# RWKV attention and SoLU feed-forward on one core: w_out's column mean taken by fp32 products of TensorE, more transposes given to DMA, and a new order of work

## The chip, the core and the metric

The kernel runs on one core of a Trainium2 chip. The core has five engines with queues of their own: PE (TensorE, matrix products; its weight loads are shown as PEld), DVE (VectorE), ACT (ScalarE), POOL (GpSimd) and SP (SyncE, which here only issues transfers). Each works through its instructions in order and waits on semaphores for the others. Products go to PSUM, which has eight banks of 512 fp32 columns by 128 partitions; everything else lies in SBUF. Transfers (DMA) are issued from SP, ACT or POOL and run on 16 DMA engines. The metric is the device time in microseconds (us) of one execution; smaller is better.

## The reference

Per batch b (4) and head h (8), over 768 steps with head size 48, a decaying state is read and updated; its output, as 3072 rows of 384, goes through a hidden layer of 1024 with a softmax-weighted activation, a layer norm with gain g, and an output product:

```python
for t in range(S):
    cur = np.einsum('bhd,bhe->bhde', u[None] * kt, vt)
    y[:, :, t] = np.einsum('bhd,bhde->bhe', rt, state + cur)
    state = wt[:, :, :, None] * state + np.einsum('bhd,bhe->bhde', kt, vt)
...
h = x @ w_in
e = np.exp(h - h_max)
sm = e / (np.sum(e, axis=-1, keepdims=True) + 1e-09)
solu = h * sm
ln = (solu - mu) / np.sqrt(var + 1e-06) * g_ln
return (ln @ w_out).astype(np.float32)
```

## The kernel before

The 768 steps are cut into 6 chunks of 128, so there are 24 units (chunk, batch), unit i being chunk i // 4 of batch i % 4. Each unit goes through the same stages, and one long string, ORDER (lines 21 to 65), says by hand-written or planned words in which order the instructions of all stages are recorded; each engine executes its own in that order. A word is a stage's letters, the unit and, after a point, an engine or a PSUM bank: `kr2.d` copies unit 2's transposed keys by DVE, `M3.0` takes unit 3's scores into bank 0. `InOrder` (line 70) keeps each engine to the order of the words, and also keeps the transfers issued from SP and ACT in one order; its line 86 records nearly all instructions, so nearly every row of the profile carries L86, and rows are told apart by what they write and read.

The stages of a unit, with the word and the line of the function:

- loads `LW`, `LK`, `LR`, `LV` (263 to 272) of w, k, r, v, 192 KB each, without a suffix from SP, with `.a` from ACT, with `.g` from POOL. Each input has a ring of seven tiles.
- `lw` (337), logarithm of w on ACT; `cum` (340), sums of it along time by two products on PE; `ex` (346), exponentials in PSUM on ACT; `kp` (350), k and r scaled by them on DVE.
- `krk`, `krr`, `kr` (388 to 394): the scaled k and r turned by eight transposes of PE and copied out of PSUM by ACT or DVE. For eleven units `kt` (398) turns them by one DMA from SP instead.
- `p`, `q`, `dg`, `dv` (354 to 375): the bonus term with u, on POOL with a sum on DVE. `vb` (367): v in bf16, on ACT or POOL.
- `M` (407), the scores, eight products; `m` (415), masked and copied out by DVE or ACT.
- `Y` (429), the output of the recurrence; with `i` the bonus is added by a product with the identity, with `n` by DVE in `y` (451), which copies it out (`.a` by ACT, `.d` by DVE). `S`, `et`, `st` (457 to 480): the state.
- `X`, `xT` (485 to 490): y turned by three transposes of PE and copied out by ACT or DVE; for seven units `xt` (401) turns it by one DMA from SP.
- `H` (497), the hidden layer, 24 products with w_in; `e` (515), exponential on ACT; `he` (527), product on DVE; `hq` (533), square on ACT; `Oa`, `Ob` (588, 592), products with w_out and the column sums for the norm; then `qm`, `lv`, `rs`, `o` and the store `out`. For four units the hidden layer is taken by rows and turned by `ht`.

Once, at the start, the weights are made ready. `LI` loads w_in in three parts, `wi` (303) casts each to bf16. `LO` loads w_out in two halves of four blocks. `gs`, `gc` (296, 300) turn and scale g. `gw` (307, `gain`) multiplies a block of w_out by g, eight times, all on ACT; `mn` (314) takes the mean over all rows of the result by eight bf16 products with a matrix of -1/1024; `ce` (322, `centre`) adds that to each block: on DVE from the fp32 block, g and the mean in PSUM in one operation, on POOL to the block already multiplied by g, from the mean that `mc` (319) has copied to SBUF. Six blocks are centred on DVE and two on POOL. Centred blocks are used first by `Oa0`. `hot` (329) issues products on zeros that keep PE active. `us` (289) spreads u over the partitions by the one fp32 product of 384 columns.

Of the kernel before, what the change touches and what calls it, by code (L numbers as in the profile page):

```python
# [8 lines left out]
F32 = mybir.dt.float32  # L9
BF16 = mybir.dt.bfloat16  # L10
# [8 lines left out]


ORDER = """
LU0 LR3.g LW3.a LW1.a LW2.g lw3 LR0.a cum3.0 LG0 ih0 ex3 LW0 gs0.7 LK3 LR2.g hot1.2 LV0.g ik0 LK0 lw1 lw0 LV3.g
gc0 cum0.4 LK2.a us0.6 p0 lw2 LW5.g ex0 kp3 LR1 kp0 cum1.0 cum2.2 krk3.7 krr3 uc0 ex2 q0 ex1 kp2 LK1 LR6.g kp1
krk0.6 LW4 krr0 krk2.5 krr2 kr0.a lw4 LR4.g vb0.a kr2.d vb3.a p1 M0.3 p3 LO0 LW6 dg0 M2.5 kr3.a LK4 m0.d lw5
hot10.1 LV1 LR5 LK6.a dv0 LK5.g m2.d LV2.a LO1 M3.0 S0.7 q3 gw2.a gw3.a hot1.4 LI1 q1 lw6 krk1.6 cum4.2 et0 LV4
m3.d p2 st0 cum6.0 dg3 gw0.a cum5.4 ex4 S3.7 gw1.a p4 kp4 q2 dv3 krr1 ex6 dg1 LV5.g krk4.3 krr4 ex5 vb1.a Y0.i2
kp6 kr4.d y0.a LI2 et3 X0.2 krk6.3 st3 p6 kr1.a vb2.a LW8 xT0.a kp5 krr6 LI0.a dg2 M1.0 krk5.7 krr5 kr6.a m1.d
S1.2 dv1 M4.4 dv2 Y3.i3 S2.6 gw4.a LK7 gw7.a et2 kr5.d LW7.g et1 m4.d hot1.7 y3.a q4 gw6.a Y1.i3 M6.0 gw5.a st2
Y2.i5 y1.a y2.a vb5.a mn0.4 X2.7 wi0.a vb4.a st1 m6.d wi1.p LR7.g M5.2 X1.0 S5.1 xT2.a S4.6 et5 p5 lw7 LR8.g dg4
ce4.d LK8 LV7 et4 ce2.d wi2.a xT1.d st5 LW10.a st4 X3.5 m5.d LR10.a cum7.0 mc0 ex7 xT3.a ce1.d H0.6 dv4 H1.2 kp7  # L30
LK9.g H3.0 e0 lw8 e1 ce0.d LK10.a he0 he1 lw10 H2.6 ce7.d hq0.a ce3.p krk7.5 ce5.p e3 LV9 e2 LK11 hq1.a ce6.d
Oa0.3 q6 he3 vb7.a krr7 Ob0 LW9.g LV6.g Y4.i4 q5 LV8.g LR9.a he2 dg5 LW11 cum10.1 cum8.6 y4.a Oa1.0 qm0 ex10 lv0
rs0 kr7.d ex8 kp10 LW13.g Ob1 krk10.4 o0.a hq3.a p8 kp8 p7 dv5 Y5.n5 qm1 LR11.g y5.d lv1 M7.2 X4.6 LW15.a m7.d
q7 krr10 LW17 dg7 kr10.d xT4.a q8 dg6 rs1 lw11 p10 Oa3.5 o1.a cum11.6 dg8 hq2.a H4.2 LW12 LR12.a ex11 lw9 kp11
out0 S7.0 et7 Ob3 dv7 Y7.n1 vb6.a out1 cum9.6 LR17 LK15.g Oa2.4 qm3 st7 vb8.p e4 Ob2 he4 lv3 dv6 LK14.g krk8.0
S6.2 X5.3 LK12.a LV10 krr8 LV12.g ex9 lw13 y7.d rs3 o3.a hq4.a kp9 lw12 qm2 Y6.i5 lv2 xT5.d X7.7 krk11.6 LV11
vb9.p out3 kr8.d krr11 LR13.g LW14.a cum12.0 et6 xT7.a y6.a rs2 LR14.g st6 M8.2 krk9.5 krr9 kr11.d ex12 m8.a
H5.6 o2.d out2 q10 M11.3 LK13 lw17 kp12 dv8 LR15 S8.0 kr9.d LV15.g M9.1 e5 m11.d Oa4.5 LW18 Ob4 m9.a sel8 he5
LV14 et8 X6.6 vb11.a M10.3 st8 xT6.d p9 lw14 cum14.1 LK17.g hq5.a ex14 qm4 lv4 m10.d cum13.6 ex13 hot2.0 q9 rs4
kp14 kp13 dg9 Y8.i0 o4.a LW21.g dg10 sel9 Oa5.4 cum17.1 S9.3 LR16 lw15 p11 ex17 S11.5 cum15.6 Ob5 kp17 y8.a p12  # L40
et9 qm5 ex15 lv5 kp15 st9 dv9 Y9.n0 q11 q12 y9.d et11 rs5 H6.1 X8.6 o5.a p13 vb12.a p14 st11 dg11 kt12 e6 out4
dv11 LK21.g H7.3 X9.5 xT8.a he6 e7 LR19.g hq6.a vb10.a H8.6 lw18 krk14.0 LV16 dg12 krr14 dv10 kt15 xT9.d out5
he7 M12.1 Oa6.5 LV13.g Y11.n4 m12.d kr14.a e8 Ob6 M15.0 y11.d qm6 LR18 hq7.a lv6 he8 rs6 m15.d H9.3 dv12 o6.a
# [3 lines left out]
lv8 vb13.p q13 e11 kp18 dv14 rs8 S15.2 o8.a S13.3 st12 e12 Oa9.0 dv15 he11 et15 lw21 LW20 Y15.n6 hq11.a et13
dg13 LV21 he12 Ob9 LV23.g LV19.g p18 st15 M13.4 LW23 y15.d qm9 dv13 kt16 cum21.1 hq12.a ex21 H10.6 lv9 p16 m13.d
st13 lw19 kp21 Y13.i4 Oa11.3 e10 rs9 o9.a out7 he10 q18 cum19.1 Ob11 dg18 qm11 lw20 Oa12.7 Ob12 ex19 LR22 q16
y13.a kp19 hq10.a M16.1 dg16 S14.5 lv11 Y14.n6 rs11 LV20.g X13.4 LV22.g out8 qm12 lv12 p17 m16.d xT13.d y14.d  # L50
o11.a lw22 S16.0 vb17.p et14 q17 dg17 rs12 st14 o12.a LR23 vb18.a cum20.1 p19 et16 ex20 ea10.p H13.3 q19 e13
# [49 lines left out]
def kernel(  # L101
# [16 lines left out]
    DM = H * D  # L118
    DF = moe_w_in.shape[1]
# [25 lines left out]
    def bank(shape, dtype, slot, name):  # L145
        size = 1
        for d in shape[1:]:
            size *= d
        first = int(slot) * 512
        if dtype == BF16:  # L150
            part = banks[:, first:first + size // 2].bitcast(BF16)
        else:
            part = banks[:, first:first + size]
        if len(shape) == 2:
            return part
        names = "abc"[:len(shape) - 1]
        return part.rearrange(f"p ({' '.join(names)}) -> p {' '.join(names)}", **dict(zip(names, shape[1:])))
# [467 lines left out]
    def store(i, x):  # L625
# [2 lines left out]

    stages = dict(
        ih=make_halves, ik=make_keep, LW=load_w, LK=load_k, LR=load_r, LV=load_v, LU=load_u, LG=load_g, LI=load_w_in, LO=load_w_out,  # L630
        us=spread_u, uc=copy_u, gs=turn_g, gc=copy_g, wi=cast_w_in, gw=gain, mn=column_mean, mc=copy_mean,
        ce=centre, hot=warm_up,
        lw=log_w, cum=cumulate, ex=decays, kp=scaled, p=bonus_rk, q=bonus_u, vb=v_cast, dg=bonus_sum, qh=bonus_half, dv=bonus_v,
        krk=transposed_k, krr=transposed_r, kr=transposed_copy, M=scores, m=scores_copy, sel=scores_mask,
# [41 lines left out]
```

## Time and profile before

| | |
|---|---|
| median of 3 runs | 144.75 us (144.69 to 145.68) |
| profiled execution | 145.05 us |
| its span, first to last instruction | 143.2 us |
| mean granted clock of TensorE | 0.995 |
| transfers turning k and r, y, hidden rows | 11, 7, 4 |
| HBM read, written | 22.03 MB, 4.72 MB |

The profile is of one execution. A group's row gives the instruction (what it writes <- what it reads), its count, the busy time and the mean ns of one, and then the idle time of its engine just before it and what ended that. A row in order of time gives start, length and the instruction. A waits row says which engine waited for whom. "The chain that ended last" follows the work back from the last instruction, at each step to what released it. Products on PE overlap: a row of 324 ns may start another every 160 ns, so the spacing of starts is the price of one and not its length. "Idle time" of an engine off the chain costs nothing by itself.

### The profile page before, as it was taken

What the parts mean: (1) busy time and instruction counts of PE and PEld (TensorE: products, weight loads), DVE (VectorE), ACT (ScalarE), POOL (GpSimd) and SP (SyncE); (2) the same over time, 40 slices, a digit from 0 to 9 for tenths busy, and PEclk for the clock granted to TensorE, in tenths of its full rate; (3) what the DMA queues carried; (4) which work ended last, traced back from release to release, by engine and by line L of the source; (5) the groups of instructions that cost most, each with busy time, mean ns of one, the idle gap of its engine ahead of it and who ended that gap; (6) DMA issues with size and microseconds to landing.
All of it is one profiled execution on the core that took longest, in us unless ns stands there. A gap on an engine that the chain in (4) does not pass through costs nothing.

```text
span 143.2 us, 4784 instructions
## 1 busy us (share of the span) xinstructions
PE 127.6 (89%) x1886; PEld 94.5 (66%) x1886; DVE 124.0 (87%) x206; ACT 122.2 (85%) x254; POOL 117.2 (82%) x150
## 2 busy tenths in 40 slices
PE   0597956988999999999999999996999999999980
PEld 0145445556967878678987797786778566687750
DVE  6048879979999999999999999999699999888480
ACT  3658799979999999999999989995787887887962
POOL 7999999999999999999999999999994753326000
PEclk9999999999999999999999999999999999999998
DMA  4999999999995999999998999996977863985325
GB/s 93 277 297 347 313 287 381 384 267 240 287 299 118 250 273 314 255 263 163 211 268 215 271 201 252 195 256 99 169 165 80 223 128 79 142 213 180 115 80 197
DMA packets 86488, 31.67 MB, mean 221 GB/s; under 512 B 80153, under 2 KB 84258, under 8 KB 86466
## 3 DMA queue, kind: packets, MB, share of 16 engines
q1 hardware_dynamic: 69330, 20.62, 66.6%
q0 software_dynamic: 2432, 7.47, 16.4%
q10 hardware_dynamic: 14704, 3.28, 10.5%
q8 instruction: 14, 0.23, 0.7%
q14 instruction: 8, 0.07, 0.1%
HBM read 22.03 MB, written 4.72 MB: 187 GB/s over the span
## 4 chain that ended last, share of the span: by engine, by line
PE 51%; POOL 21%; ACT 8%; issue 7%; DVE 5%; DMA 4%; ACTq 0%; POOLq 0%; DVEq 0%
PE ps L86 51%; DMA xT<-y 4%; POOL kr_in L86 4%; POOL p L86 4%; POOL q L86 3%; POOL dv L86 2%; POOL v_in L86 2%; ACT hq L86 2%; POOL w_in L86 2%; ACT e L86 2%; DVE he L86 1%; DVE o L86 1%; ACT o L86 1%; ACT ps L86 1%; DVE m L86 1%
## 5 line engine op out<-in xcount | busy, mean ns | idle before, releaser
L86 PE MATMUL ps<-w,he 128*128 128x386 bf16 (+1 forms) x192 | 42.5, 324 | 0.0
L86 PE MATMUL ps<-xT,win_sb 128*128 128x128 bf16 x480 | 29.6, 219 | 1.4 <-DMA xT<-y 1.2
L86 PEld LDWEIGHTS <-win_sb 128*128 128x128 bf16 x480 | 27.4, 98 | 3.0 <-DMA xT<-y 1.3
L86 POOL TENSOR_TENSOR dv<-vb,dg 128x384 bf16<-128x384 bf16 x24 | 19.8, 829 | 11.8 <-DVE dg L86 8.6
L86 DVE TENSOR_TENSOR kp<-ps,kr_in 128x768 bf16<-128x768 f32 x24 | 22.7, 953 | 6.9 <-DMA kr_in<-in_r_dram 3.8
L86 ACT ACTIVATE e<-ps 128x1024 bf16<-128x1024 f32 (+1 forms) x25 | 24.6, 987 | 4.8 <-PE ps L86 3.8
L86 DVE TENSOR_TENSOR m<-ps,keep 128x1024 bf16<-128x1024 f32 x22 | 26.7, 1218 | 0.9 <-PE ps L86 0.9
L86 DVE TENSOR_TENSOR he<-ps,e 128x1024 bf16<-128x1024 f32 (+1 forms) x21 | 24.5, 1170 | 3.0 <-ACT e L86 2.8
L86 PE MATMUL ps<-one_col,hq 128*128 128x1 bf16 x160 | 26.1, 163 | 0.0
L86 POOL TENSOR_TENSOR p<-kr_in 128x384 bf16<-128x384 f32 x24 | 23.9, 1005 | 0.1
L86 POOL TENSOR_TENSOR q<-p,u_bc 128x384 bf16<-128x384 bf16 x24 | 21.8, 916 | 0.3
L86 PEld LDWEIGHTS <-he 128*128 128x128 bf16 x192 | 18.3, 96 | 4.0
L86 ACT ACTIVATE hq<-he 128x1024 bf16<-128x1024 bf16 (+1 forms) x20 | 20.7, 1033 | 0.0
L86 ACT ACTIVATE ps<-ps 128x768 f32<-128x768 f32 x24 | 19.0, 800 | 1.5 <-PE ps L86 1.4
L86 PEld LDWEIGHTS <-hq 128*128 128x128 bf16 x160 | 14.1, 96 | 8.8
L86 PE MATMUL ps<-inv_col,e 128*128 128x2 bf16 x104 | 17.1, 164 | 0.0
L86 ACT ACTIVATE lw<-w_in 128x384 bf16<-128x384 f32 x24 | 12.3, 519 | 4.2 <-DMA w_in<-in_w_dram 4.2
L86 PEld LDWEIGHTS <-kp 128*128 128x128 bf16 x184 | 12.3, 101 | 4.2 <-DVE kp L86 1.9
L86 PEld LDWEIGHTS <-kr 64*128 64x128 bf16 (+1 forms) x272 | 10.2, 95 | 5.3 <-issue 2.1
L86 DVE TENSOR_REDUCE dg<-q 128x8 f32<-128x384 bf16 x24 | 12.9, 543 | 0.0
L86 DVE TENSOR_TENSOR st<-ps,et 128x384 bf16<-128x384 f32 x20 | 10.8, 551 | 1.4 <-ACT et L86 1.4
L86 POOL DMA_DIRECT2D v_in<-in_v_dram x12 | 10.9, 905 | 0.0
(97 smaller groups left out, 284.9 us busy)
## 6 DMA issues: line engine op xcount, KB each, us to landing
out_dram<-o SPq DMA_DIRECT2D x24, 192.0 KB, 2.7
w_in<-in_w_dram SPq DMA_DIRECT2D x12, 192.0 KB, 5.6
kr_in<-in_k_dram SPq DMA_DIRECT2D x12, 192.0 KB, 5.9
v_in<-in_v_dram POOLq DMA_DIRECT2D x12, 192.0 KB, 4.9
kr_in<-in_r_dram POOLq DMA_DIRECT2D x11, 192.0 KB, 4.5
v_in<-in_v_dram SPq DMA_DIRECT2D x11, 192.0 KB, 4.3
kr_in<-in_r_dram SPq DMA_DIRECT2D x9, 192.0 KB, 4.0
wout_f<-in_moe_w_out_dram SPq DMA_DIRECT2D x2, 768.0 KB, 7.1
```

Of the source, the lines that this page charges most:

```text
L86: made = make(*args, **kwargs)
```

## The change

Gain and mean. The eight `gw` words, `mc` and the bf16 matrix `mean_w` go. `copy_g` makes a second copy of g, scaled by -1/1024. `mn` becomes two words, one for each half of w_out: four products each, with fp32 operands, the moving one being the loaded block and the stationary one a column of that copy repeated 128 times. All eight blocks are centred on DVE in the operation that six used before. (The POOL form of `centre` is rewritten too, but no word uses it.)

Transposes. `kt` turns k and r for thirteen units (8 and 10 are new), `xt` turns y for thirteen (9, 10, 11, 12, 16 and 22 are new); the words `krk`, `krr`, `kr` and `X`, `xT` of these go.

Other words. w_in is cast by POOL three times (before: ACT twice, POOL once). The kr copies are eight on ACT and three on DVE (before five and eight), y copies six and eighteen (before nine and fifteen), x copies four and seven (before nine and eight), outputs seventeen and seven (before eighteen and six), v casts fourteen on ACT and ten on POOL (before sixteen and eight). The halved exponential sums `ea` on POOL are eight (before seven), and three `Y` more go without the identity product. Loads of units from ACT: 23 (before 14); from POOL: 33 (before 38); from SP: 40 (before 44). The long warming word `hot10` stands ahead of the first sums instead of behind the third scores. The rows that are turned (`ht`) are units 16, 18, 20 and 21 (before 17 to 20). The order of all words is another, line by line.

```diff
-    mean_w = consts.tile([128, 128], BF16)
-    dve.memset(mean_w, -1.0 / DF)
...
+    gm = consts.tile([128, KF], F32)
...
     def copy_g(i, x):
         act.mul(out=gr, in_=ps["g"], mul=RDF * EPS)
+        act.mul(out=gm, in_=ps["g"], mul=-RDF * EPS / DF)
...
-    def gain(f, x):
-        if x == "a":
-            act.activation(out=w2[:, f, :DM], in_=wout_f[:, f, :], func=COPY, scale=gr[:, f:f + 1])
-        else:
-            (dve if x == "d" else pool).tensor_scalar(out=w2[:, f, :DM], in0=wout_f[:, f, :],
-                                                      scalar1=gr[:, f:f + 1], scalar2=None, op0=MULT)
-
-    def column_mean(i, x):
-        ps["mean"] = bank([128, DM], F32, x, "mean_ps")
-        for f in range(KF):
-            pe.matmul(ps["mean"], lhsT=mean_w, rhs=w2[:, f, :DM], start=(f == 0), stop=(f == KF - 1))
+    def column_mean(j, x):
+        first = "mean" not in ps
+        if first:
+            ps["mean"] = bank([128, DM], F32, x, "mean_ps")
+        for f in range(j * KF // 2, (j + 1) * KF // 2):
+            pe.matmul(ps["mean"], lhsT=gm[:, f:f + 1].to_broadcast([128, 128]), rhs=wout_f[:, f, :],
+                      start=(first and f == j * KF // 2), stop=(not first and f == (j + 1) * KF // 2 - 1))
...
     def centre(f, x):
         if x == "p":
-            pool.tensor_add(out=w2[:, f, :DM], in0=w2[:, f, :DM], in1=mean_sb)
+            pool.scalar_tensor_tensor(out=w2[:, f, :DM], in0=wout_f[:, f, :], scalar=gr[:, f:f + 1], in1=mean_sb,
+                                      op0=MULT, op1=ADD)
```

The new order around the start of the hidden layers, with the two words of the mean and the centrings (the words `LO1`, `LI2`, `LI0`, `LO0` and `LI1` stand ahead of this, in that order):

```
dg2 m4.d krk6.3 p6 dg4 krr6 dv2 kr5.a mn1.7 dg3 kr6.a M6.1 wi2.p y2.d m6.d LW8.a dv3 M5.4 wi0.p S3.0 LW7.a X0.6
Y3.i3 LW11 mn0.4 m5.d ce4.d xT0.a X1.4 ce5.d LR10.g LR7.a ce1.d wi1.p LV10 ce2.d LR8.a X2.2 vb5.a H0.5 y3.a X3.3
```

More of the change, by code (lines that the diff above doesn't have):

```diff
@@ L27 @@
[L27 to L31, printed above, removed]
@@ L47 @@
[L47 to L51, printed above, removed]
@@ new lines @@
+Y3.i3 LW11 mn0.4 m5.d ce4.d xT0.a X1.4 ce5.d LR10.g LR7.a ce1.d wi1.p LV10 ce2.d LR8.a X2.2 vb5.a H0.5 y3.a X3.3
+et3 p5 ce3.d st3 ce6.d xT2.a xT1.a LV7.a dv4 xT3.d lw7 ce7.d e0 LV6.g cum7.0 S5.2 q5 LW9 LK8 ex7 LW12.g LK10.a
+H1.3 he0 lw10 ce0.d q6 vb10.p LV8 lw8 et5 LR13 H2.5 LV11.g kp7 e1 krk7.0 LR11.a LK12 hq0.a e2 he1 krr7 LK13.a
+st5 Y4.n7 p7 y4.d cum10.3 hq1.a H3.1 LV9 ex10 Oa0.7 e3 kr7.d vb7.p he2 lw11 LW14 X4.6 Ob0 kp10 cum8.4 dg5 Oa1.0
+ex8 qm0 LK9.g lw12 S7.3 LR9.g he3 LK11.g LV12.a M7.1 hq2.a lv0 dv5 LR12.a Ob1 LV17.g kp8 xT4.d vb6.p q7 cum11.5
@@ new lines @@
+kt8 et7 rs0 m7.d o0.a ex11 qm1 p8 dg7 Oa2.4 hq3.a S6.7 p9 st7 H4.1 et6 lw9 lv1 Y5.n3 kp11 st6 dg6 Ob2 cum9.6
+LW17.a e4 y5.d rs1 he4 o1.a ex9 dv7 q8 qm2 LW15.g dv6 kp9 Oa3.5 X5.0 krk11.2 q9 xT5.d krr11 p10 Ob3 dg9 hq4.a
+LK14 out1 lv2 dg8 qm3 LW13.a q10 cum12.0 kr11.a rs2 ex12 vb9.p Y6.i7 Y7.n6 vb8.a out0 LV14.a o2.d krk9.2 y7.d
+lv3 y6.a lw17 p11 kt10 q11 rs3 kp12 LK16 dg10 dv8 krr9 LV13.g LR18 M8.3 kr9.d LR17.a LR14 LK17.g LV15 m8.a H5.6
+dg11 vb11.p o3.a M11.3 out3 M9.1 lw14 m11.d Oa4.5 e5 S8.0 X7.3 he5 m9.a et8 lw13 xT7.d Ob4 X6.4 qm4 st8 cum14.1
@@ new lines @@
+hq5.a sel9 dv11 p12 M10.6 S9.3 xT6.d lv4 lw15 et9 ex14 LK15.a dv9 sel8 Y9.n0 out2 p14 rs4 Oa5.4 m10.d cum13.6
+o4.a Ob5 LR16.g q14 kp14 st9 LW21 vb14.a cum17.1 LR15.a ex13 dv10 y9.d S11.3 ex17 et11 kp13 Y8.i5 Y11.i0 qm5
+y8.a lv5 y11.a rs5 kt12 cum15.6 xt9 ex15 q12 kp17 lw21 X8.5 p17 H6.1 o5.d e6 st11 kp15 H7.3 vb12.a e7 xT8.d H8.5
+e8 krk14.0 he6 out4 dg14 Y10.n7 krr14 kr14.a LW16.g LK18 S10.2 et10 LR19.g LR21 LW20.g hq6.a he7 he8 H9.3 vb15.a
+ea7.p kt15 p13 e9 vb13.a M12.0 dg12 S12.6 hot1.5 Oa6.5 y10.d q13 Ob6 dv12 m12.d LW18 st10 p15 Y12.n7 lw16 LV16
@@ new lines @@
+q15 M15.1 he9 M14.3 LW19.g y12.d qm6 m15.d hq8.a out5 hq7.a lv6 rs6 vb16.a S15.0 Oa8.7 xt11 LK19.g et15 LV18
+m14.d dg13 Ob8 o6.a kt13 hq9.a qm8 xt12 dv14 et12 lv8 S13.2 rs8 et13 cum16.4 Oa7.3 LK21 p16 lw18 st15 Ob7 st12
+o8.d LW22.g ex16 cum18.0 p18 H11.6 dg15 ex18 kp16 qm7 q16 st13 H12.4 lv7 xt10 Oa9.2 rs7 LK20.g kp18 dv15 e11
+o7.a LK22 ea11.p dg16 he11 Y15.n3 e12 ea12.p Ob9 kt16 cum21.0 LR20.g he12 dv13 out8 q17 M13.4 qm9 hq11.a q18
+H10.6 y15.d lw19 LR22.g Y14.n3 lv9 out7 ex21 m13.d kt17 hq12.a Oa11.5 Ob11 kp21 LV19 M16.0 e10 rs9 dv16 y14.d
@@ new lines @@
+he10 cum19.3 vb18.a qm11 xt15 o9.a p19 LV20.g ex19 m16.d Y13.n7 Oa12.6 lv11 Ob12 kt18 y13.d S16.2 kp19 rs11 dg18
+LW23 qm12 X13.4 o11.a hq10.a et16 vb17.p st16 xT13.d lw20 q19 lv12 dg17 Y16.n7 out9 rs12 LV22.g out11 y16.d
+S14.5 o12.a et14 st14 LV23 dg19 out6 lw22 cum20.0 xt14 ex20 H13.2 H15.6 dv18 e13 kp20 cum22.0 S17.4 he13 e15
+Oa10.5 M18.2 ex22 Ob10 he15 hq15.a kp22 m18.d hq13.a qm10 H14.6 M17.0 kt19 m17.d e14 lv10 Oa13.3 rs10 Ob13 p20
+vb20.p Y17.n0 o10.a dv17 S18.5 he14 kt20 hq14.a kt21 xt16 LR23 y17.d Y18.n2 ea15.p et17 xt17 p21 q20 et18 dg20
@@ new lines @@
+out12 M19.6 y18.d qm13 ea14.p Oa15.0 Ob15 lv13 q21 LK23.g st17 st18 vb19.a qm15 rs13 m19.d vb22.a o13.a lv15
+H16.1 lw23 rs15 xt18 M20.4 o15.a e16 dg21 m20.d out13 H17.6 dv20 S19.0 Oa14.3 cum23.4 he16 Y20.n2 out10 e17 sv16
+ex23 Ob14 he17 kt22 LV21.g y20.d et19 M21.6 kp23 hq17.a vb21.a p22 dv19 hq16.a m21.d q22 H18.1 dg22 ht16 ea17.p
+kt23 dv21 Y19.n5 X20.4 e18 y19.d Y21.n7 Oa16.6 y21.d xt19 Ob16 xT20.a M22.4 he18 sq16 st19 p23 m22.d vb23.p
+hq18.a qm14 lv14 qm16 dv22 Oa17.7 ht18 H20.0 Y22.n2 lv16 y22.d e20 Ob17 H19.4 rs16 rs14 he20 o14.a M23.0 q23
@@ new lines @@
+qm17 xt21 dg23 sv18 o16.a e19 ea19.p xt22 Oa18.6 hq20.a Ob18 out14 m23.d lv17 Y23.n2 rs17 ht20 out15 he19 out16
+dv23 sq18 hq19.a H21.0 o17.d e21 H22.4 y23.d qm18 Oa19.3 lv18 rs18 he21 xt23 Oa20.7 e22 hq21.a Ob20 he22 sv20
+sq20 Ob19 HA23.1 hq22.a EA23 qm19 qm20 o18.d lv20 lv19 HB23.0 rs20 ht21 DA23 EB23 rs19 ea22.p sv21 o20.d out17
+Oa22.2 Ob22 o19.a Oa21.1 Ob21 QA23.a qm22 lv22 sq21 DB23 QB23.d Oa23.4 qm21 Ob23 out18 lv21 rs21 out20 rs22
+o22.d qm23 o21.a lv23 rs23 out19 out21 o23.a out22 out23
@@ L630 @@
         ih=make_halves, ik=make_keep, LW=load_w, LK=load_k, LR=load_r, LV=load_v, LU=load_u, LG=load_g, LI=load_w_in, LO=load_w_out,
-        us=spread_u, uc=copy_u, gs=turn_g, gc=copy_g, wi=cast_w_in, gw=gain, mn=column_mean, mc=copy_mean,
+        us=spread_u, uc=copy_u, gs=turn_g, gc=copy_g, wi=cast_w_in, mn=column_mean, mc=copy_mean,
         ce=centre, hot=warm_up,
```

39 lines of the change are left out of this document (6 added, 33 removed).

## The prediction

> **What bounds the kernel now.** I read the page's busy shares first, then the chain of work that ended last, then a table of busy time by stage, then the rows of the stages that the change touches.
>
> ```profile
> span 143.2 us, 4784 instructions
> PE 127.6 (89%) x1886; PEld 94.5 (66%) x1886; DVE 124.0 (87%) x206; ACT 122.2 (85%) x254; POOL 117.2 (82%) x150
> ...
> PE 51%; POOL 21%; ACT 8%; issue 7%; DVE 5%; DMA 4%; ACTq 0%; POOLq 0%; DVEq 0%
> ```
>
> Four engines are within 10 us of each other, so the share of busy time decides nothing. The chain in order of time does: POOL carries it from 2.7 to 39, ACT from 39 to 46.8, then PE without a gap to 88, one transfer from 92.5 to 98.7, PE again to 130.1, and a mixed tail to the end.
>
> ```profile
> 10.00:20.00 10.00, 8.48 (x93) 5.37 (x90) 8.39 (x10) 8.42 (x16) 9.94 (x12) 1.00 1.17 315
> 20.00:30.00 10.00, 7.65 (x127) 5.38 (x125) 9.98 (x15) 9.11 (x20) 9.96 (x12) 1.00 1.12 362
> 30.00:40.00 10.00, 8.85 (x147) 7.59 (x142) 9.17 (x15) 9.99 (x18) 9.66 (x12) 1.00 1.13 262
> ...
> 46.80:130.10 83.30, 82.12 (x1316) 63.52 (x1316) 79.58 (x122) 74.46 (x155) 70.44 (x83) 1.00 0.97 204
> ```
>
> The columns are the length, the busy time of PE, PEld, DVE, ACT and POOL, the granted clock, the DMA share and GB/s. Up to 40, PE has room (5 us of 30 idle) while POOL, DVE and at the end ACT are full. From 46.8 to 130.1 PE is idle 1.2 us of 83.3, DVE 3.7, ACT 8.8. So PE sets the pace there with DVE 2.5 us behind it.
>
> ```profile
> 7.33 1.64 PE L86 MATMUL ps<-u_row,ones_row 1*128 1x384 f32 x2
> ...
> 28.20 1.47 PE L86 MATMUL ps<-w,mean_w 128*128 128x384 bf16 x8
> ...
> 33.26 0.91 PE L86 MATMUL ps<-xT,win_sb 128*128 128x128 bf16 x9 [0.16 <-DVE st L86]
> ```
>
> The first row is the only fp32 product of 384 columns, two records; the second is the eight bf16 products of w_out's mean; the third is the first hidden layer, H0, at 33.26. ACT's last cast of w_in runs from 32.50 to 33.55, right there, behind ACT's eight multiplications by g:
>
> ```profile
> L86 ACT ACTIVATE w<-wout_f,gr 128x384 bf16<-128x384 f32 x8 | 4.6, 621 | 0.6 <-issue 0.6
> L86 POOL DMA_DIRECT2D v_in<-in_v_dram x12 | 10.9, 905 | 0.0
> L86 POOL TENSOR_TENSOR w<-w,mean_sb 128x384 bf16<-128x384 bf16 x2 | 1.6, 826 | 0.3 <-ACT mean_sb L86 0.3
> L86 DVE SCALAR_TENSOR_TENSOR w<-wout_f,gr,ps 128x384 bf16<-128x384 f32 x6 | 3.5, 608 | 0.0
> ```
>
> And the one transfer on the chain, a y turned by DMA:
>
> ```profile
> 92.53 6.12 DMA xT<-y
> ```
>
> **The change part by part.** I split at H0, since both orders have the same seven scaled units, seven score blocks and 10.22 MB of loads before it. A word's price is the spacing of its instruction's starts in the trace, which is up to 0.1 us under its duration.
>
> *ACT before H0:* eight multiplications by g go (8 x 0.52), two casts of w_in go to POOL (1.9), the copy of the mean goes (0.4), two casts of v go to POOL (0.8), an exponential and a logarithm move behind H0 (1.15), so do two x copies and two y copies (1.6), two more kr copies come (1.9), gm costs 0.1: -8.4 us. *DVE before H0:* two kr copies fewer (1.2), two state updates and an x copy later (1.2), one centring (0.5) and one y (0.5) more: -1.4. *POOL before H0:* four issues of loads fewer at 0.9, one p later (0.96), two v casts (0.9) and two w_in casts (1.96) more: -1.7. The issues that POOL loses go mostly to ACT, where they took 0.35 to 0.60 each and lay beside running work except once (0.65 us at 16.5); eight more over the whole run cost ACT nothing to 5 us, and its 8.4 us cover that.
>
> *PE before H0:* the fp32 mean comes in, eight products, sixteen records. The trace has none at full speed with 128 rows. The row above gives 0.79 a record (7.33 to the next start at 8.91), taken while bf16 products of 384 columns stood 0.27 to 0.32 apart; from 17.58 on they stand 0.16 apart. Nearest is that row halved for the rate, 0.39: 6.3 us. Ends: 12.6 at the unhalved price, and below the 1.3 of bf16 nothing speaks for a gain; 1.3 to 12.6. In place of the 1.3 now, and less 1.2 of other work moved behind H0, that is +4.1 (21.5 after 17.5), and PE had 5 us of idle time from 10 to 40. The ten warming products, 2.3 us at 14.24 now, move to the very start, where PE waits until 4.09 anyway; they can hold up the first sums by some 1 us, but the unit's keys and r, issued second on POOL instead of first, land about 0.9 later too, so that costs nothing beyond those 0.9, and the fourth unit's scaling, ended at 13.2 now by ACT's late logarithm at 8.70, need not be later.
>
> The Trainium skill (FP8 and Floating Point Precision, TensorE Precision Notes) speaks against this step: true fp32 takes four passes through the array. An estimate by it is 8 x 4 x 0.16 = 5.1 us, where the halved row gives 6.3; the trace agrees in kind, since its two records together cost five bf16 products.
>
> That the change does not do what it says can be left out: the built order has two groups of four fp32 products and no ACT instruction that reads w_out.
>
> *When H0 comes.* Transfers: by the table 217, 315 and 362 GB/s moved 8.9 MB by 30. w_out's second half ends the first 7.9 MB of the new order, about 27.2. Four products (3.15) end the mean at 30.4, and H0 can follow at 30.8. w_in's last block lands by about 28.7 and POOL's cast ends by 29.7. POOL's work says 33.26 - 1.7 = 31.5. I take POOL's, the later: **-1.7**. Ends: -2.5 (30.8) and +0.6 (mean at 12.6: 27.2 + 6.3 + 0.4 = 33.9).
>
> *PE behind H0:* two kr turned by DMA (16 transposes, 0.9), five x (0.9), two y sums without the identity product (0.3), one more state and one more pair of decay sums (+0.8), the rest small: -1.6. *DVE behind H0:* three kr copies fewer (1.8), two state updates (0.9), two y (0.9), one centring (0.5), one output (0.5) more: +1.1. *ACT* +0.2, *POOL* -0.4. PE's lead over DVE of 2.5 us is used up by 1.6 + 1.1, so DVE becomes an equal bound and the gain on PE is not had whole: between 0 and -1.6, taken half, **-0.8**.
>
> *Transfers turned by DMA.* Two more kr, six more y. SP issues them in order: 7.75 us more on its queue, at 1.25 each. In the trace (tile views) a y took 2.3 to 6.1 us to land, a kr 3.2 to 5.7; SP was held 1.2 to 3.6 us by one. Of seven y, one stopped PE, for 1.2 us; of eleven kr, none did. Queued behind a waiting one on SP are later loads and the stores; loads have their ring of seven units ahead. At the rate of the trace six more y cost 6 x 1.2 / 7 = **+1.0**; ends nothing and 7.2 (each stops PE).
>
> Sum: -1.7 - 0.8 + 1.0 = -1.5. The profiled execution took 145.05 (143.2 and 1.85 around it), so 143.55; the median of the three runs is 0.3 lower, so **143.2**.
>
> **Rivals.** *PE keeps the whole gain* (DVE follows, as it had 3.7 us of idle time, and no transfer is late): -2.5 - 1.6 = -4.1, 140.6. For it: ACT is relieved by 8.2 us in all, POOL by 2.1. Against: DVE was at 96% from 46.8 to 130.1.
>
> *DVE is the bound, no gain:* centring started at 30.0 with 100.6 us of DVE work left; now the mean ends at 30.4 with 99.9 left: -0.3, 144.4. For it: DVE's total falls by 0.3 only (122.6 to 122.3).
>
> *The fp32 mean stops PE's queue:* behind it stand the scores of units 6 and 5, and DVE's masks and the centrings wait for these. At 0.79 a record the mean ends at 33.5 and DVE's remaining 99.9 start 3.5 us later than 30.0: +2.8, 147.5. It decides from about 0.5 a record on (DVE's part +0.6). Against: every bf16 row halves after 14 us.
>
> *Turned y come late (the other side):* y 9 to 12 are now turned between 60 and 90, where the DMA share is already 1.03 to 1.12 and loads still flow; SP issues more than twice as many transposes there (14 in place of 4 before H13). If four of them stop PE as the one at 92.53 did, by 1.2 to 2.5 us (the products' and weight loads' waits of 1.2 and 1.3 together), that is +4.8 to +10 in place of +1.0, with -2.5 from the rest: +2.3 to +7.5, about 148. It decides from three stops on. Against: the new order leaves 2.7 to 5.7 us of PE work between the turning word of y 9 to 12 and its hidden layer, where the seven of the old one have 0 to 4.2.
>
> The Trainium skill (DMA: Bandwidth & Descriptors, Latency and other measured facts) gives 261 GB/s for a transpose with a strided middle; an estimate by it is 0.4 us for a y of 98 KB and 1.0 for a kr of 262 KB, far under the landing times here, so by it the extra 1.1 MB would not fill the engines, and what is late would be the queue.
>
> **How the numbers follow.** Forecast case 0.48 (142.2 to 144.3), PE's whole gain 0.16, DVE the bound 0.18, the mean 0.06, late y 0.12. About 1% is what a measurement of this kernel can tell from no change: 143.3 and 146.2. The forecast is split in half by 143.3, so faster is 0.26 + 0.16 = 0.42, same 0.22 + 0.18 = 0.40, slower 0.18. The range runs from 140.9, near the first rival's end, to 147.0, which leaves out most of late y and the mean's upper end.
>
> **What would show it.** Sixteen fp32 records at about 0.39 spacing, two groups of four products, the second ending near 30.4; H0 at 31 to 32; no ACT rows out of wout_f; ACT near 114 busy. From H0 to 130 DVE idle under 3 us, PE's waits on xT transfers at 1 to 2 in number. Wrong if H0 comes after 33, if PE waits for turned y over 3 us in all, or if DVE waits at the centrings over 2 us.

## The result, and the profile after

In 20 runs of each kernel the changed one took 148.57 us in the median (145.58 to 153.11) and the one before 145.05 (143.91 to 148.05). The ratio is 1.0114 with a 95% interval of 1.0067 to 1.0161; in a second series of runs it was 1.0197 (1.0136 to 1.0259). So the change makes the kernel slower by 1 to 2% by these ratios, and by 2.4% by the two medians, where I forecast 1.5 us off. The ratios take the executions within 1.5% of each kernel's fastest (five of the changed kernel's twenty), and as its profiled one (150.31) was not among them, a second profile of the same program, of an execution of 147.34 with a span of 145.6, is read beside it; the sum is settled on that one.

The busy rows of the second profile, to set against those of before (127.6, 94.5, 124.0, 122.2, 117.2):

```profile
span 145.6 us, 4706 instructions
PE 130.4 (90%) x1853; PEld 95.4 (66%) x1853; DVE 123.0 (84%) x205; ACT 115.0 (79%) x236; POOL 115.3 (79%) x148
```

ACT lost 7 us of the 8 that I had forecast, POOL 2, DVE 1; PE gained 3. The same four stretches as before, second profile (length, busy PE, PEld, DVE, ACT, POOL, granted clock, DMA share, GB/s):

```profile
10.00:20.00 10.00, 8.00 (x93) 5.12 (x91) 9.41 (x12) 7.52 (x16) 9.52 (x19) 0.86 1.22 274
20.00:30.00 10.00, 8.29 (x118) 5.93 (x119) 7.58 (x12) 5.98 (x13) 8.38 (x10) 1.00 1.04 345
30.00:40.00 10.00, 8.09 (x101) 6.34 (x100) 8.10 (x14) 6.22 (x13) 8.85 (x12) 1.00 1.24 279
46.80:130.10 83.30, 81.56 (x1300) 62.41 (x1297) 79.83 (x123) 73.67 (x155) 73.43 (x84) 1.00 1.06 209
```

The head is emptier on DVE and POOL too, not only on ACT: from 20 to 40 DVE worked 15.68 us where it had 19.15, POOL 17.23 for 19.62. POOL waited 2.6 us of it for two blocks of w_in to land. What DVE waited for stands on PE, in order of time (second profile):

```profile
25.99 2.85 PE L85 MATMUL ps<-wout_f,gm 128*128 128x384 f32 x8 [0.93 <-DMA wout_f<-in_moe_w_out_dram]
28.77 0.62 PE L85 MATMUL ps<-kr 64*128 64x128 bf16 x16
...
30.65 2.85 PE L85 MATMUL ps<-wout_f,gm 128*128 128x384 f32 x8 [0.33 <-DMA wout_f<-in_moe_w_out_dram]
33.33 0.50 PE L85 MATMUL ps<-ident,y 128*128 128x128 bf16 x6
33.67 1.50 PE L85 MATMUL ps<-xT,win_sb 128*128 128x128 bf16 x24
```

The first row is the first fp32 group, the second the scores of units 6 and 5 (`ps<-kr`) behind it, the third the second group, which waits for w_out's second half, and the last H0 behind it all. The chain of this stage names the transfer:

```profile
21.69 8.91 DMA wout_f<-in_moe_w_out_dram
30.60 0.04 issue
30.65 2.86 PE ps L85 x8
33.51 0.03 issue
33.53 2.71 DVE w L85 x5
```

Some marks, from rows in order of time (`e` is the exponential of a hidden layer):

| start of | before | second profile | first profile |
|---|---|---|---|
| first centring | 30.00 | 33.53 | 32.27 |
| H0 | 33.26 | 33.67 | 32.41 |
| e0 | 35.05 | 35.86 | 35.24 |
| e9 | 75.37 | 76.47 | 75.23 |
| e13 | 97.56 | 100.14 | 103.50 |
| end of the span | 143.2 | 145.6 | 148.6 |

The second profile is 1.1 us behind at e9 and 2.4 at the end. The first is level at e9 and then loses 6.1 us on the kernel before by e13, at this transfer:

```profile
74.96 3.54 SPq L85 DMA_DIRECT2D out_dram<-o  x1
79.04 2.25 SPq L85 DMA_TRANSPOSE xT<-y  x1
81.40 0.52 SPq L85 DMA_DIRECT2D v_in<-in_v_dram  x1
81.97 2.20 SPq L85 DMA_TRANSPOSE kr<-kp  x1
84.27 1.20 SPq L85 DMA_TRANSPOSE xT<-y  x1
```

y 12 was ready near 78.5, but the last of these five rows is its transpose; it landed at 88.28, and PE stood 3.0 us. What follows the stop is in the stretches of the first profile:

```profile
84.00:88.00 4.00, 1.38 (x24) 1.20 (x22) 3.98 (x6) 2.41 (x5) 3.96 (x6) 1.00 1.07 198
88.00:92.00 4.00, 3.67 (x46) 2.98 (x47) 0.81 (x2) 1.83 (x2) 1.57 (x2) 0.67 1.08 236
92.00:96.00 4.00, 4.00 (x69) 3.03 (x67) 3.00 (x5) 2.78 (x6) 3.98 (x6) 0.90 0.80 150
```

The clock is 0.67 and 0.90 in the eight microseconds behind the stop, 4 x 0.33 + 4 x 0.10 = 1.7 us of PE's work. (It is one piece at half clock, from 89.4 to 92.8.)

### The profile page after: what moved, and what is told of

The parts are those of the page before. It is cut to its first block, busy times and chain, and to the rows that moved or that the text cites. A ratio compares the mean times of both kernels' runs of the same rounds, so it can differ in the third digit from the quotient of the medians.

```text
span 148.6 us, 4706 instructions
## 1 busy us (share of the span) xinstructions
PE 131.9 (89%) x1853; PEld 96.2 (65%) x1853; DVE 123.3 (83%) x205; ACT 114.8 (77%) x236; POOL 115.5 (78%) x148
## 4 chain that ended last, share of the span: by engine, by line
PE 43%; DVE 14%; POOL 14%; DMA 13%; issue 8%; ACT 5%; DVEq 0%; POOLq 0%
PE ps L85 43%; DMA w_in<-in_w_dram 7%; DMA xT<-y 6%; POOL p L85 4%; POOL dv L85 3%; POOL q L85 3%; DVE he L85 3%; DVE m L85 3%; DVE w L85 3%; DVE kp L85 2%; ACT hq L85 2%; DVE st L85 1%; POOL vb L85 1%; ACT lw L85 1%; POOL m L85 1%
## 5 line engine op out<-in xcount | busy, mean ns | idle before, releaser
L85 PE MATMUL ps<-w,he 128*128 128x386 bf16 (+1 forms) x192 | 43.5, 330 | 0.0
L85 ACT ACTIVATE ps<-ps 128x768 f32<-128x768 f32 x24 | 18.9, 799 | 3.7 <-PE ps L85 3.7
L85 POOL TENSOR_TENSOR ea<-e 128x512 bf16<-128x512 bf16 x8 | 9.2, 1155 | 15.3 <-ACT e L85 15.3
L85 PEld LDWEIGHTS <-he 128*128 128x128 bf16 x192 | 18.2, 97 | 4.4
L85 PE MATMUL ps<-inv_col,e 128*128 128x2 bf16 x96 | 16.1, 167 | 0.0
L85 PEld LDWEIGHTS <-kr 64*128 64x128 bf16 (+1 forms) x272 | 10.8, 96 | 6.0 <-issue 3.2
L85 PEld LDWEIGHTS <-kp 128*128 128x128 bf16 x168 | 11.2, 102 | 2.4 <-ACT u_bc L85 0.5
L85 PE MATMUL ps<-lw,uti_neg 128*128 128x384 bf16 x24 | 8.3, 346 | 3.9 <-ACT lw L85 2.3
```

Of the source, the lines that this page charges most:

```text
L85: made = make(*args, **kwargs)
```

## The experiments

Theory A: DVE loses the head, waiting for the fp32 mean, which ends late. Theory B: the six new turned y stop PE. Rivals: the clock or ACT's load issues hold the head; SP's load as such. Words were edited in ORDER, the rest of each kernel left alone (`mean_two`, `both_undone` and `before_mean` also change the functions of the mean); "profile" below is the one profiled execution of each.

**Six y back on PE** (`y6_on_pe`).

```
- xt9 ... xt11 ... xt12 ... xt10 ... xt16 ... xt22
+ X9.0 xT9.a ... X11.2 xT11.a ... X12.1 xT12.a ... X10.1 xT10.a ... X16.1 xT16.a ... X22.3 xT22.a
```

> The changed kernel, but the six y that are newly turned by DMA (9, 10, 11, 12, 16, 22) go back to three PE transposes and an ACT copy each, at the place where the transfer was issued; all other words are the changed kernel's. Theory late y (the new transfers queue on SP, land late and stop PE in the middle, as the 3.0 us before the hidden layer of unit 12, after which PE runs at half its clock for some 4 us): no wait of PE on a turned y between 80 and 95, the granted clock stays 1.00 there, exponentials of units 12 and later come 3 to 5 us earlier than in the changed kernel, the whole 144 to 146 us. Rival head (what is lost is lost ahead of the ninth hidden layer, by the mean and by ACT held at loads): the time stays that of the changed kernel, 146 to 149, since six x add 1.1 us of PE work. Rival both sides of the order (the order was planned around these transfers, so PE's place for the x is as bad): 147 to 150.

147.64 us (146.79 to 148.57), ratio 1.0152 (1.0103 to 1.0202). The spread falls from 7.5 us (20 runs) to 1.8 (6 runs) and no stop for y is left between 80 and 95; but the kernel is not faster than the changed one at its best, and still slower than before. B explains the upper times, not the lower ones.

**The six transfers left out** (`no_y6`): the same six words deleted.

> The changed kernel with the turning of y 9, 10, 11, 12, 16 and 22 left out altogether (their hidden layers read whatever the buffer held; nothing else changes). Theory 'late y' (the six transfers stop PE and SP): PE's waits on xT between 75 and 95 fall to nothing, the scatter shrinks as with those y on PE, and the time falls by the 1.1 us that PE and ACT spend on them there: 146 to 146.7 in the median. Theory 'head' (the loss lies before e1 and the transfers are free): 147.5 to 148.5, as the changed kernel.

146.58 (145.03 to 149.29), ratio 0.9981 (0.9926 to 1.0036). Against `y6_on_pe` it saves the 1.1 us of the turning on PE (2.5 by the two ratios); against the second series of the changed kernel (148.07) 1.5, and 3 by the two ratios (0.0216 x 145). So the six transfers cost 1.5 to 3 us over many executions, where I had priced them at 1.0. Its profile (an execution of 147.61) shows nothing of that behind e9: from there to the end it takes 69.3 us, with none of the six, where the second profile takes 69.1 and the kernel before 67.8.

**The six y by DMA in the kernel before** (`before_y6_dma`): X and xT of those y deleted, `xt` put right behind each y.

> The kernel before, but y 9, 10, 11, 12, 16 and 22 are turned by DMA, issued from SP right behind the word that copies y; nothing else is changed. Theory late y: SP's queue, now with six more transfers between 60 and 125 us, brings at least one hidden layer late, PE waits 2 us or more for turned y in 70 to 95 and its clock is seen to fall there; 147 to 150 us. Rival (the transfers as such are harmless, it is the new order that puts them badly or something else that costs): 143.5 to 145.5, since 1.1 us of PE's transposes go.

165.22 (162.86 to 169.33), ratio 1.1239 (1.1172 to 1.1305). PE and its loads waited for turned k and r, not for y (profile, waits):

```profile
PEld L86 <- DMA kr<-kp: 14.0, 7, 4.5
...
PE ps L86 <- DMA kr<-kp: 12.2, 5, 4.1
```

An `xt` issued before its y is ready stands on SP and holds back every transfer behind it: SP issued nothing from 62.4 to 67.5, where y 9 was ready, and the turned k and r behind it went out at 68.8 where before they went out at 61.4.

**Turned y 11 and 12 issued first** (`xt_first`).

```
- LV16 ... out5 ... xt11 LV18 kt13 xt12
+ LV16 ... xt11 xt12 out5 ... LV18 kt13
```

> The changed kernel with two words moved on SP: the turning of y 11 and 12 stands ahead of a store of outputs, a load of v and a turned k, r pair in place of behind them. Theory 'late y by the queue': the transposes are issued at about 75 and 78.5 in place of 77.6 to 79 and 82.3 to 84.3, H12 does not wait, no half clock follows, PE's waits on xT before 95 are under 1 us: 146 to 147 with a small scatter. Theory 'the transfers are slow wherever they stand': waits stay near 3 us and the time at 148. If only the place of the stop moves (to kr 13), PE waits on kr instead.

152.69 (149.98 to 158.03), ratio 1.0247 (1.012 to 1.0374). H12 did not wait any more (its exponential at 88.27; 87.96 in the second profile, 90.17 in the first), but y 10 and later ones came late: PE waits of the profile from 62 to 125:

```profile
PE ps L85 <- DMA xT<-y: 8.2, 3, 3.9
```

The stop moves, and grows.

**Which of the six** (`y1112_on_pe`, `y_rest_on_pe`): y 11 and 12 alone on PE, or the other four alone.

> The changed kernel with y 11 and 12 alone turned by PE and copied by ACT again, the other four by DMA. If the stop at H12 makes the upper heap of times: one heap, 146.5 to 148.5, no PE wait on xT over 1.2 us between 80 and 95. If any of the six can stop PE, SP's queue being full from 60 to 100 (18.5 and 18.9 of 20 us in the changed kernel, 14.4 and 18.9 before): two heaps stay, 147 and 150 to 152.

> The complement: y 9, 10, 16 and 22 turned by PE, y 11 and 12 by DMA. If the stop at H12 makes the upper heap: times up to 150 to 152 stay and some trace shows PE waiting 2 to 3 us at about 85, with the granted clock under 0.9 behind it. If SP's load as a whole does it: one heap at 147 to 148.5, since two transposes fewer stand between 60 and 80.

149.0 (148.05 to 150.49), ratio 1.0237 (1.0162 to 1.0313), and 148.99 (146.72 to 152.8), ratio 1.0164 (1.0054 to 1.0274). With y 11 and 12 on PE the stop came at H17 instead (PE's row, profile of `y1112_on_pe`), and the clock fell as well:

```profile
114.53 2.74 PE L85 MATMUL ps<-xT,win_sb 128*128 128x128 bf16 x24 [2.10 <-DMA xT<-y]
```

```profile
112.00:116.00 4.00, 1.90 (x24) 1.71 (x24) 2.99 (x4) 1.57 (x3) 1.85 (x3) 0.81 1.06 172
116.00:120.00 4.00, 4.00 (x55) 3.23 (x54) 1.61 (x2) 1.93 (x5) 1.15 (x1) 0.77 0.61 138
```

The 24 products of a hidden layer take 1.50 us elsewhere and 2.74 here. In the profile of `y_rest_on_pe` H12 waited 3.2 us, and from e9 to e13 it took 29.3 us where the second profile takes 23.7. Not one y, but any that comes late, and not only by SP's queue: y 17, which stopped H17, is turned by DMA in the kernel before too; here SP issued its transfer as soon as y was ready (108.64), and it took 5.8 us to land, where before it took 2.3. SP issued for 18.5 of 20 us from 60 to 80 and 18.2 from 80 to 100 in the first profile, 14.3 and 18.9 before, 16.5 and 11.7 with the six on PE.

**The mean with two products** (`mean_two`): a loop over one block of each half.

```
- for f in range(j * KF // 2, (j + 1) * KF // 2):
+ for f in (j * KF // 2,):
```

> The changed kernel with one fp32 product a half in place of four: six of the mean's eight products are left out, 4.1 us of PE in the head at 0.34 a record. If the products themselves cost (PE sets the head's pace): the centrings start 2 us earlier than 32.3 to 33.5 and e4 comes 2 to 4 us earlier, time 144 to 146. If w_out's second half landing near 30.6 and ACT's held load issues set the head: the centrings start at 31 or later, e0 stays at 35 to 36 and the time stays within 1 us of the changed kernel's.

Its profiled execution took 146.34, 1.0 under the changed kernel's second; DVE's two waits for PE all but went (from 10 to 36; first the changed kernel's second profile, then this one's):

```profile
DVE m L85 <- PE ps L85: 1.9, 1, 1.9
DVE w L85 <- PE ps L85: 1.9, 1, 1.9
```

```profile
DVE m L85 <- PE ps L85: 0.8, 2, 0.6
...
DVE w L85 <- PE ps L85: 0.2, 1, 0.2
```

(Before, DVE waited 0.4 us for m and not at the centrings.) The centrings began at 30.56, against 33.53 and 32.27 in the two profiles of the changed kernel; e4 came at 49.99, against 51.51 and 50.26 (before: 49.66), and e9 at 75.50, against 76.47 and 75.23. So the waits are the mean's, but without them this execution is ahead of the second profile alone and not of the first: that six products fewer gain anything in the end is not shown. H0 now ran into the next limit, POOL's cast of w_in's last block, and then ran at half clock (0.50 from 32.3 to 35.7):

```profile
30.77 0.22 PE L85 MATMUL ps<-xT,win_sb 128*128 128x128 bf16 x1
32.06 2.44 PE L85 MATMUL ps<-xT,win_sb 128*128 128x128 bf16 x23 [1.07 <-POOL win_sb L85]
```

In the time it is not settled either: the median of four runs is 149.91 (146.34 to 150.63), and turned y are still there.

**The mean behind the scores** (`y6_mean_behind`), on top of `y6_on_pe`.

```
- kr5.a mn1.7 dg3 ... M5.4 wi0.p
+ kr5.a dg3 ... M5.4 mn1.7 wi0.p
```

> The changed kernel with all six y on PE and the first group of fp32 products moved behind the scores of units 6 and 5 on PE's queue (nothing left out). If the place of the group ahead of the scores costs: DVE's wait of 1.1 to 1.9 for m goes, the mean still ends at 32.5 to 34, the time is 0.5 to 1 under the 147.6 of the kernel with six y on PE. If the mean's end alone decides, DVE waits as much longer at the first centring (3 us in place of 2) and the time stays within 0.4 of 147.6.

149.93 (149.35 to 150.5), ratio 1.0328 (1.0253 to 1.0403), 2.3 over `y6_on_pe`:

```profile
DVE w L85 <- PE ps L85: 4.1, 1, 4.1
...
DVE m L85 <- PE ps L85: 0.2, 1, 0.2
```

The wait for m goes and the one at the centring grows past it. The scores themselves came only 0.5 us earlier (27.23), as they now waited for ACT's copy of kr, and the mean ended at 34.1 where it ended at 32.2 in `y6_on_pe`. Neither case of the expectation held: 1.9 us later for the mean are 2.2 at e9 (77.57 for 75.38) and 2.3 in the time. This is the cleanest sign of A: what the mean lost here, the kernel lost.

**The mean and centring alone, in the old order** (`before_mean`).

```
- gw0.a ... gw7.a ... vb5.a mn0.4 X2.7 ... mc0 ... ce3.p ... ce5.p
+ m4.d mn0.4 hot1.7 ... vb5.a mn1.0 X2.7 ... ce3.d ... ce5.d
```

> The kernel before with the change of the mean alone: no multiplications by g on ACT and no copy of the mean, two groups of four fp32 products (the first 10 words ahead of the old place, the second at it), all eight blocks centred on DVE; all other words of the old order. Theory head (the fp32 mean and the centring on DVE are a loss there: PE +4 us, DVE +1.0 ahead of the hidden layers): the first exponential comes later than 35.05 and the whole is 146 to 148. Rival (the step itself pays, ACT ahead of H0 loses 4.6 us and POOL 1.6; what is lost is lost by the new order and the transfers): first exponential at 33 to 35, the whole 143 to 145.

151.16 (149.83 to 156.12), ratio 1.0391 (1.0322 to 1.0459). e0 came 4.8 us later than before (39.81); DVE waited 4.5 us for m and 1.0 at the centrings. So the mean and the centring, at the places given to them here, cost 5 us with no new order and no new transfer; the new order, whose e0 comes at 35.24 and 35.86, makes most of that good.

**w_out's second half loaded earlier** (`lo0_early`).

```
- LO1 LI2 lw4 lw5 LI0 lw6 LO0
+ LO1 LO0 LI2 lw4 lw5 LI0 lw6
```

> The changed kernel with the load of w_out's second half issued right behind the first half, ahead of two blocks of w_in (five words earlier on SP). If the late landing (30.6 where I took 27.2) ate the head's gain: the second group of fp32 products ends at 29 to 31, the centrings start 2 us earlier, e0 at 34 to 35, and the time falls by 1 to 2 us. If ACT's held issues and POOL set the head, e0 stays at 35 to 36 and the time stays at 147.5 to 148.5; if the two w_in blocks then land late, e0 comes later.

149.09 (147.61 to 152.23), ratio 1.0171 (1.0086 to 1.0255). The first group starts 0.8 earlier than in the second profile (25.15; 25.08 in the first), but the second at 30.57 (30.65 and 29.39), now behind a product that waited 1.08 us for POOL:

```profile
30.20 0.32 PE L85 MATMUL ps<-dv,ident 128*128 128x384 bf16 x1 [1.08 <-POOL dv L85]
30.37 0.36 PE L85 MATMUL ps<-vb,m 128*128 128x48 bf16 x8
30.57 2.83 PE L85 MATMUL ps<-wout_f,gm 128*128 128x384 f32 x8
```

So the landing at 30.6 was not the only thing that held the mean; PE's own queue can hold it to the same time.

**Rivals for the head** (`loads_off_act`: LR7, LR8, LV7 from SP; `stay_warm`: twelve products on zeros behind `cum2`; `stores_on_act`: eleven stores issued from ACT to relieve SP).

> The changed kernel, but the loads of r of units 7 and 8 and of v of unit 7 are issued from SP at the same places instead of from ACT, where they took 2.93 us (two) and 1.78 us at 29 to 34 us while ACT stood still. Theory head (ACT held by a load's issue that waits for the transfer eight before it eats what ACT gained): ACT is not idle for 2.6 us at 29.5 to 32.1, the first exponential comes 0.8 to 1.5 us earlier than at 35.2, and the whole gains 0.5 to 1.5 us on the changed kernel if nothing behind takes it back. Theory late y: the first exponential may move, the time of the whole stays within 1 us of the changed kernel's, because SP's queue and the hidden layer of unit 12 set the middle.

> The changed kernel with twelve more products on zeros right behind the first unit's sums, so that PE does not stand still from 5 to 7.6 us. In the changed kernel the granted clock is 1.00 up to about 7 us and then a half until about 14. Theory clock (standing still after the early warming throws the clock back, and the first keys are turned at half rate): the clock stays 1.00 from 5 to 16 us, products of 384 columns stand 0.16 apart there, the first exponential of a hidden layer comes up to 1.5 us earlier than at 35.2. Rival (that stretch is paced by loads, ACT and DVE): the clock stays up and the first exponential stays within 0.4 us of 35.2, the whole is the changed kernel's.

> The changed kernel, but the stores of units 2 to 12 are issued from ACT at the same words instead of from SP, where one held the queue from 74.96 to 78.5 us (it waits for its output) with turned y 11 and 12 behind it; y 12 was issued at 84.27 although it had been copied out by 78.6. Theory head of SP's queue (a store that waits holds up the turned y): y 12 is issued before 82, PE does not wait for it, the whole is 144.5 to 147 and scatters less. Rival (SP is simply full of transposes at 2 to 3.5 us each, or they land late because the DMA engines are full): y 12 comes as late, time as the changed kernel's.

148.91 (146.01 to 152.19), ratio 1.0105 (1.002 to 1.0189); 152.22 (151.36 to 154.46), 1.0435 (1.0389 to 1.0481); 150.22 (147.78 to 151.84), 1.0274 (1.0186 to 1.0363). ACT did stand for its own issues (second profile: two r loads from 30.08 to 32.97, the second issued 0.1 us after w_in's last block had landed at 32.0, and the cast of v behind them):

```profile
30.08 2.89 ACTq L85 DMA_DIRECT2D kr_in<-in_r_dram  x2
33.01 0.51 ACT L85 CAST vb<-v_in 128x384 bf16<-128x384 f32 x1 [2.54 <-issue]
```

Taken off ACT, the wait goes and e0 stays (35.44); its profile has a stop of 3.1 us at 83.0 for a turned k and r. With twelve products more the clock is 0.97 to 1.00 from 5 to 12 (0.68 from 8 to 12 in the second profile), but the half clock only moves, to 11.7 to 15.2; e0 stays too (35.79), and the time goes to three stops for turned y, 6.6 us in all. So ACT's issues do not set the head, and the clock there was shifted and not removed; that it is not the cause shows rather in the first profile, at half clock for 6.8 us from 7.5 on and level at e9, and the second, for 3.4 us and 1.1 behind. With the stores on ACT y 12 went out at 82.45 (84.27 and 82.26 in the two profiles), PE still waited 3.4 us for turned y in three, and y 17 again took 5.7 us to land.

**Two checks on sums.** `y6_kr2_on_pe` also puts the two new k, r pairs back on PE; `both_undone` joins `y6_on_pe` and `mean_two`; `after_again` is the second profile.

> The changed kernel with all new transposes taken back: the six y as in the first run of this kind, and k and r of units 8 and 10 by eight PE transposes each and an ACT copy. PE gets 0.9 us more of work, SP 4 to 6 us less of queue. Theory transfers (what is left over the kernel before, 1.5%, is still SP's queue and the landing of transposes): 145 to 146.5, below the run with the six y alone. Rival order (it lies in the new order itself, not in the transposes): 147.5 to 149, the run with the six y alone plus PE's 0.9.

> The changed kernel with all six y on PE and two of the mean's eight fp32 products (six are left out). If DVE's wait for the mean (1.0 to 1.3 us of the time) and the turned y are the whole loss: 146.0 to 146.8 in one heap, DVE busy 23 us or more of the 26 from 10 to 36, and what is left over before is the 1.1 us of PE work for the six y. If there is a third loss: 147.5 or more.

> The changed kernel again, to have it on the same chip as these and a profile of another execution. If the late y at the hidden layer of unit 12 is in every execution, the same wait of 3 us stands there; if late y are a matter of chance (the scatter is 145.6 to 153.1), it stands at another unit or nowhere, and the time goes with the sum of PE's waits for turned y and the time at half clock behind them.

150.7 (149.78 to 151.8), ratio 1.0369 (1.0297 to 1.0441): it was 1.1 us behind `y6_on_pe` at e0 and 4.9 at e6, so the two k, r pairs do better by DMA. `both_undone`: 148.36 (147.51 to 150.43), ratio 1.0195 (1.0122 to 1.0269), not the 146 to 146.8 that A and B together would give. PE worked only 17.94 of the 26 us from 10 to 36 there and was granted 0.93 of the clock from 36 to 62, and H0 waited 1.2 us for the cast of w_in's last block, as in `mean_two`: so a third loss came in with the missing products. Whether A and B are the whole loss stays open.

**The lesson turned on the kernel before** (`before_y15_pe`): `xt15` replaced by `X15.5 xT15.a`.

> The kernel before with y 15 alone turned by PE and copied by ACT instead of DMA. If a turned y costs what its stop costs: PE's wait of 1.2 at 98.7 goes, 0.2 of PE and 0.5 of ACT come, SP gets 1.2 us free: 1.0 under before, 144 to 144.6 where before has 145 to 145.6. If the stop only moves to the next late transfer (kr 17 or y 14): within 0.4 us of before.

147.52 (146.56 to 150.67) beside 147.35 on that chip, ratio 1.0143 (1.0055 to 1.0231). The stop of 1.2 us became one of 1.7 behind ACT's copy. No kernel here beat the one before by more than the noise.

## Why the prediction was wrong

*The head, -1.7: wrong, and it is the step that failed first.* I put the mean's end at 30.4, from w_out's second half landing at 27.2 with four products right behind it, and H0 at 31.5 by POOL's work. The half landed at 29.3 in the first profile and 30.6 in the second, the mean ended at 32.2 and 33.5, and H0 came at 32.41 and 33.67: -0.9 and +0.4 instead of -1.7. The landing was not all that the sum left out. The first group cannot start before the first half is there (24.9 and 25.9), takes 2.8 us, and some 1.4 us of scores, sums and transposes stand between the groups in PE's order, so that the second could not have started before 29.2 and 30.3. And w_in's last block, which I had at 28.7, landed at 30.7 and 32.0: with the mean shortened H0 waited for its cast until 32.1. The row price was not at fault: the sixteen records took 5.7 us against 6.3.

I had also asked when H0 comes, and not when the centrings start. From 36 to 62 all engines were full before (PE 25.88 of 26 us, DVE 25.56, ACT 25.55, POOL 25.57); now DVE alone is (25.77; PE 24.66, ACT 24.30, POOL 23.86), so what DVE misses earlier it cannot make up there. What it did from 10 to 36, and when the first centring began, order most of the profiles by their e9:

| | DVE busy, 10 to 36 | first centring | e9 |
|---|---|---|---|
| before | 23.60 | 30.00 | 75.37 |
| `mean_two` | 23.26 | 30.56 | 75.50 |
| `both_undone` | 23.14 | 30.41 | 78.25 |
| `stores_on_act` | 22.70 | 32.03 | 76.48 |
| changed, first profile | 22.58 | 32.27 | 75.23 |
| `y6_on_pe` | 22.51 | 32.25 | 75.38 |
| `y1112_on_pe` | 22.35 | 32.14 | 75.95 |
| `y_rest_on_pe` | 22.35 | 32.25 | 76.37 |
| `stay_warm` | 22.28 | 32.53 | 75.69 |
| `loads_off_act` | 21.94 | 32.58 | 77.23 |
| `y6_kr2_on_pe` | 21.86 | 32.67 | 80.03 |
| `no_y6` | 21.59 | 32.84 | 76.55 |
| `lo0_early` | 21.25 | 33.43 | 76.28 |
| changed, second profile | 21.09 | 33.53 | 76.47 |
| `xt_first` | 20.80 | 33.72 | 76.93 |
| `y6_mean_behind` | 20.52 | 34.16 | 77.57 |
| `before_mean` | 18.97 | 35.44 | 81.08 |

Down to 22.5 little is lost, since by my sum the new order has 1.4 us less for DVE to do ahead of H0; below it most lose some 0.7 to 1.3 for each missing microsecond. These are single executions, and an order is no proof: `both_undone`, `y6_kr2_on_pe`, `loads_off_act` and `stores_on_act` lost more behind 36, where DVE worked 23.75, 23.34, 25.08 and 25.50. Of my signs of being wrong, H0 after 33 came true in the second profile (33.67) and turned y over 3 us in the first (3.9); DVE's wait at the centrings stayed just under 2 (1.9), with 1.9 more for m.

*PE behind H0, -0.8: wrong.* PE does have less to do, but from e0 to e9 (busy 40.2 us before, 38.9 in the second profile), where DVE is the bound; from e9 on it has more (62.4, 63.2). So none of it could be had. The rival "DVE is the bound, no gain" had this part right.

*Turned y, +1.0: too large in a quiet execution, too small in others.* The second profile loses 1.1 us by e9 and 1.3 from e9 to the end (69.1 against 67.8), together the 2.4 of the spans. Of the 1.3, PE's waits for turned y are only 0.2: 1.4 us in three, where before there were 1.2 in one. The other 1.1 stands in `no_y6` as well, which turns none of the six. From e9 to e13 PE is busy 23.3 of 23.7 us in the second profile (`no_y6`: 23.1 of 23.5; before: 22.2 of 22.2), so the new order has about 1 us more of PE's own work in that stretch, and does not get it back by the end; no run takes this apart, and the cause stays open. In other executions one late y costs 3 us of stop and 1.7 of clock; I had priced a stop by itself, with nothing behind it. The rival "turned y come late" gave 148 and asked for three stops; one long one is enough.

*The rival on the fp32 mean* had the mechanism (behind it the scores, DVE's masks and the centrings), and a wrong condition: it said that it decides from 0.5 us a record on. At 0.34 the mean was late all the same, because the products could not start when I had them start. That its 33.5 for the mean's end is the second profile's is luck: it took 0.79 a record from 27.2, and it was 0.34 from 30.6.

*Sums that do not add up as written:* ACT's list before H0 gives -8.0 and not -8.4, PE's +3.8 and not +4.1, and eight transfers at 1.25 us are 10 and not 7.75 on SP; no term of the forecast hangs on them.

*Right:* no ACT row reads w_out; two groups of four products; ACT at 115; POOL 115; the eight more issues on ACT, which cost it 2.5 us at one place and the end nothing.

The Trainium skill (FP8 and Floating Point Precision, TensorE Precision Notes) counts four passes for true fp32, an estimate of 5.1 us by the spacing of bf16 products; the trace agrees: sixteen records 0.34 apart are 5.4 us, nearer to it than to my 6.3.

## What to carry to other kernels

Ask of a stage which engine is full in it, and cost a change by when that engine gets its inputs: work taken off ACT and POOL in this head bought nothing, while DVE waited for a sum that ended 2.6 to 3.8 us later than before (at 32.2 and 33.5 for 29.7). A product that must wait for a load stands in an in-order queue with everything behind it, so a landing time from mean bandwidth needs its own bounds (here it came 2.1 and 3.4 us later), and so does the place of the product in its own queue. A transfer that replaces a cheap operation is priced by the queue that issues it and by the spread of its landing: with SP issuing 18 of 20 us, and landings of the same y between 2.3 and 5.8 us, any of them may be the late one. And an order this tight has little slack: seven of the sixteen edits raised the median by over 1% over the kernel that they edit, and only the one that leaves the six transfers out lowered it by as much, so that an undone part is read in the stage where it acts, and not by the total alone.

## What the runs showed of the hardware

An fp32 product of 128 x 128 by 384 columns is two records, 0.34 us apart at full clock (eight in 2.85 us), where a bf16 one is 0.16. The granted clock falls to a half for pieces of 3.4 us (89.4 to 92.8 in the first profile), and the length of a stop does not tell when. Stops of 3.0, 3.2 and 2.1 us had one behind them (stretches of four microseconds at 0.67, 0.77 and 0.77), stops of 2.6 and 2.8 us in `stay_warm` had none, and in `before_y15_pe` the clock fell with no stop over 1 us: PE was busy 1.72 of the 3.4 us from 19.4 on, and the next 3.4 ran at 0.51. The Trainium skill (TensorE: Matmul & The Clock Gate, Part 1) has the clock halved after an idle window of about 3.4 us; the piece of 3.4 us agrees, but none of these stops was that long, so for the cause the measurement decides. Two issues of loads from ACT held ACT for 2.5 us, the second of them until 0.1 us after a block of w_in, issued from SP, had landed. A y of 98 KB turned by DMA landed 2.3 to 6.8 us after its issue.
